# Windowed attention and two gated feed-forward blocks on one core: the order of the evacuations, the first two slices as one group, the softmax normalisation on GpSimd

## The chip, the cores and the metric

The program runs on one core of one Trainium2 chip. The metric is device time in microseconds (us) of one execution; lower is better. The engines are named as the profile names them: PE (TensorE matmul) and PEld (its weight loads), DVE (VectorE), ACT (ScalarE), POOL (GpSimd), SP (SyncE, which here issues all the DMAs).

## What is computed

```python
def _attn_ref(q, k, v):                       # (4, 8, 576, 64)
    scores = np.matmul(q, k.transpose(0, 1, 3, 2)) / np.sqrt(D)
    bias = slopes[:, None, None] * (-np.abs(rel))      # per head
    mask = (rel >= 0) & (rel < 128)
    scores = np.where(mask, scores + bias, -1e9)
    attn = np.exp(scores - max); attn = attn / (sum + 1e-9)
    return np.matmul(attn, v)
def _moe_ref(x, w_gate, w_val, w_out):        # x (2304, 512), d_ff 1536
    return sigmoid(x @ w_gate) * (x @ w_val) @ w_out
def _moe2_ref(x, w1, w2, w3, w_out):          # d_ff 1024
    return ((x @ w1) * (x @ w2) @ w3) @ w_out
```

The reference runs attention, then the first feed-forward block, then the second.

## The kernel before, in words

**Tiles and blocks.** The 2304 tokens are 18 tiles of 128, cut into five blocks of 2, 4, 4, 4 and 4 tiles (`TILES`). Attention runs over 20 steps, block by block and four head pairs in each: steps 0 to 3 are the block of two tiles (half steps), steps 4 to 19 are full. Feed-forward weights are cut into slices of 128 columns: 12 of the first block, 8 of the second. High and low halves of an fp32 value are multiplied in three passes (`PASSES`), so a product of one slice with one block is 12 matmuls, and what follows each product on ACT, DVE and POOL makes the next operand's halves.

**One attention step n** has three stages. `stage_s` multiplies queries and keys (tile `s`), then, for each pair of tiles, DVE merges the two windows (L446), adds the table of biases (L449) and takes the row maxima (L455); ACT does four exponentials with row sums (L462), DVE the reciprocals (L466), and the four 128x128 parts are scaled by them, two on POOL (L470) and two on ACT (L472). `stage_p` transposes the result on PE (L480, tile `pt`), ACT copies it to SBUF (L69, tile `cp`), POOL cuts it into two windows by two selects for each head (L484, L488). `stage_pv` multiplies by the values (L503), ACT and DVE make the halves of `xt`. On PE the stages of three steps are interleaved: p of n-2, pv of n-3, s of n.

**Fillers.** Behind the stages of a step PE gets pieces of the first feed-forward block (`fill`, a budget of PE time for each step, `FILL` and `FULL`). `READY` says at which step which group of slices on which block joins the queue of fillers. `layer` runs `gv` (the gate product, its sigmoid on ACT at L257, the value product, DVE's multiply at L262, ACT's high half at L264, POOL's low half at L265) and leaves the down product (`down1`) to the next layer; each down product is added into `acc` (L287 by ACT for the first group, L289 by DVE later). All of these share four PSUM banks with `pt` and `pv` until the attention is over.

**Order of the work.** PE's order inside the attention is written out by hand (`tc.manual_schedule`). The order on ACT, DVE, POOL and SP comes from a scheduler: it follows the program's order, shifted by `tc.high_priority(offset=...)`. Weights are converted on the way (`convert_next`, one at a time, L115 to L121 and L131 to L135) at an offset of -300. Each engine works off its own list strictly in order.

**Groups before.** `groups` begins with (0,) and (1,), single slices, then pairs. After the attention three layers of the single slices are left, then the pairs run over the five blocks, one after the other, to the end of the kernel.

## Time and profile before

| | |
|---|---|
| median of 3 runs | 945.8 us (945.59 to 946.12) |
| the profiled execution's own time | 945.88 us |
| its span, first to last instruction | 944.2 us |
| busy: PE, DVE, ACT, POOL | 897.6, 573.5, 366.9, 290.6 us |
| mean granted TensorE clock | 0.979 |

A busy share is an average over stages with different limits. Here the span falls into an attention of some 200 us, in which all engines work on short pieces in turn, and 740 us of feed-forward matmuls. A row of the timeline is start, duration, engine and line, and in brackets how long the engine had been idle before and what ended it; "x8" merges eight like instructions, and PE shows two records for an fp32 matmul of the attention. The granted clock is given in tenths or as a share of 2.4 GHz, so 0.5 is 1.2 GHz.

### The profile page before, as it was taken

To read this page: it belongs to the slowest core of one execution; us is meant where nothing else is said; L and a number is where in the kernel's file an instruction comes from. 1 tells how busy PE (TensorE), PEld (TensorE's weight loads), DVE (VectorE), ACT (ScalarE), POOL (GpSimd) and SP (SyncE) were. 2 spreads that over 40 slices of the span, in tenths; PEclk is the share of its full clock that TensorE was granted. 3 is DMA by queue.
4 is the path that set the end of the run, shared out by engine and by line. 5 is a ranking of instruction groups with operands and counts; after the bars stand their busy time and mean duration, and the time that the engine had idled before them with its cause. 6 is when DMAs were issued, how large, how long until landed. Compare 5 with 4: busy or idle time off the path is not lost.

```text
span 944.2 us, 12323 instructions
## 1 busy us (share of the span) xinstructions
PE 897.6 (95%) x4528; PEld 736.6 (78%) x4528; DVE 573.5 (61%) x957; ACT 366.9 (39%) x912; POOL 290.6 (31%) x343
## 2 busy tenths in 40 slices
PE   6788786899999999999999999999999999999998
PEld 3456665678878888888888888888888888888887
DVE  5769686525998797698593458943854514422223
ACT  6799897643333332322331244434322312211110
POOL 4567454242422412322322021104422412411111
PEclk9789898999999999999999999999999999999999
DMA  6445353114243243143130122325310300000112
GB/s 185 150 140 161 99 159 119 40 34 145 79 143 113 67 135 101 45 144 113 45 100 23 46 67 101 112 78 156 97 39 1 112 1 1 23 0 1 45 45 112
DMA packets 32604, 79.71 MB, mean 84 GB/s; under 512 B 3616, under 2 KB 5664, under 8 KB 32544
## 3 DMA queue, kind: packets, MB, share of 16 engines
q1 hardware_dynamic: 32544, 78.92, 26.0%
q8 instruction: 36, 0.59, 0.3%
q14 instruction: 24, 0.20, 0.1%
HBM read 65.27 MB, written 13.63 MB: 84 GB/s over the span
## 4 chain that ended last, share of the span: by engine, by line
PE 73%; DVE 11%; ACT 8%; DMA 4%; issue 4%; POOL 1%; SPq 0%; ACTq 0%; POOLq 0%; DVEq 0%
PE gv L243 43%; PE dn L280 11%; PE o L304 10%; PE w3o L209 4%; ACT sm L462 3%; PE pv L503 2%; DVE acc L289 1%; PE s L438 1%; PE pt L480 1%; ACT sm L472 1%; DVE sm L449 1%; DVE s L446 1%; DVE mn L455 1%; ACT cp L69 1%; POOL wsl L75 1%
## 5 line engine op out<-in xcount | busy, mean ns | idle before, releaser
L243 PE MATMUL gv<-xt,wsl 128*128 128x512 f32 (+1 forms) x1440 | 307.6, 372 | 3.2 <-DVE g L262 1.9
L243 PEld LDWEIGHTS gv<-xt,wsl 128*128 128x128 f32 x1440 | 252.5, 191 | 52.7 <-DVE g L262 3.0
L75 POOL TENSOR_TENSOR gt<-g,gt 128x512 fp32r<-128x512 f32 (+1 forms) x100 | 120.5, 1209 | 430.1 <-ACT gt L69 422.8
L243 PE MATMUL gv<-x,wsl 128*128 128x512 f32 (+1 forms) x960 | 200.2, 368 | 0.0
L243 PEld LDWEIGHTS gv<-x,wsl 128*128 128x128 f32 x960 | 167.6, 189 | 30.2
L262 DVE TENSOR_TENSOR g<-g,gv 128x512 f32<-128x512 f32 (+1 forms) x100 | 62.6, 630 | 168.1 <-PE gv L243 151.1
L280 PE MATMUL dn<-gt,wsl 128*128 128x512 f32 (+1 forms) x720 | 156.3, 371 | 5.0 <-ACT cp L69 3.1
L280 PEld LDWEIGHTS dn<-gt,wsl 128*128 128x128 f32 x720 | 126.4, 189 | 30.1 <-ACT cp L69 3.7
L257 ACT ACTIVATE g<-gv 128x512 f32<-128x512 f32 (+1 forms) x100 | 54.7, 550 | 156.1 <-PE gv L243 150.9
L69 ACT ACTIVATE gt<-g 128x512 fp32r<-128x512 f32 (+1 forms) x100 | 58.5, 587 | 145.4 <-DVE g L262 145.2
L304 PE MATMUL o<-wsl,gt 128*128 128x512 f32 x432 | 101.1, 389 | 0.0
L304 PEld LDWEIGHTS o<-wsl,gt 128*128 128x128 f32 x432 | 80.9, 188 | 16.7
L289 DVE TENSOR_TENSOR acc<-acc,dn 128x512 f32<-128x512 f32 (+1 forms) x120 | 74.1, 628 | 21.8 <-PE dn L280 21.5
L313 DVE TENSOR_TENSOR acc<-acc,o 128x512 f32<-128x512 f32 x54 | 37.1, 688 | 35.2 <-PE o L304 35.2
L462 ACT ACTIVATE sm<-sm,mn 128x128 f32<-128x128 f32 x144 | 55.9, 391 | 1.6 <-DVE mn L455 1.0
L503 PE MATMUL pv<-cp,ldv 128*64 128x256 f32 (+1 forms) x352 | 43.4, 382 | 12.6 <-issue 6.9
L503 PEld LDWEIGHTS pv<-cp,ldv 128*64 128x64 f32 x352 | 27.1, 154 | 29.2 <-issue 12.9
L438 PE MATMUL s<-ldk,ldq 64*128 64x256 f32 x288 | 42.1, 434 | 6.3 <-DMA ldq<-in_q_dram 6.3
L470 POOL TENSOR_SCALAR sm<-sm,su 128x128 f32<-128x128 f32 x72 | 32.6, 464 | 41.4 <-DVE su L466 41.4
L209 PE MATMUL w3o<-wo,w3s 128*128 128x512 f32 x192 | 44.4, 390 | 0.2 <-DVE wo L72 0.2
L209 PEld LDWEIGHTS w3o<-wo,w3s 128*128 128x128 f32 x192 | 36.0, 188 | 8.1 <-DVE wo L72 0.7
L438 PEld LDWEIGHTS s<-ldk,ldq 64*128 64x128 f32 x288 | 29.5, 209 | 14.1 <-issue 10.6
(742 smaller groups left out, 868.7 us busy)
## 6 DMA issues: line engine op xcount, KB each, us to landing
ldk<-in_k_dram SPq DMA_DIRECT2D x16, 320.0 KB, 3.0
ldv<-in_v_dram SPq DMA_DIRECT2D x16, 320.0 KB, 2.9
out_dram<-acc SPq DMA_DIRECT2D x18, 256.0 KB, 2.0
ldq<-in_q_dram SPq DMA_DIRECT2D x16, 256.0 KB, 3.3
w3o<-w3os SPq DMA_DIRECT2D x8, 256.0 KB, 2.5
ldk<-in_k_dram SPq DMA_DIRECT2D x4, 128.0 KB, 2.9
ldq<-in_q_dram SPq DMA_DIRECT2D x4, 128.0 KB, 3.0
raw_(0, 0)_99<-in_w_gate_dram SPq DMA_DIRECT2D x1, 512.0 KB, 4.6
```

The source lines that it names most:

```text
L69: nc.scalar.activation(dst, src, AF.Copy)
L75: nc.gpsimd.tensor_tensor(dst, src, hi.bitcast(F32), ALU.subtract)
L209: nc.tensor.matmul(acc2, w3s[u][:, wp, i * P : (i + 1) * P], wo2[kk][:, xp], start=(kk == 0 and wp == 0 and xp == 0), stop=(kk == NC2 - 1 ...
L243: nc.tensor.matmul(ps, wsl[i][:, s, wp, kk * P : (kk + 1) * P], xs[blk][:, xp, kk], start=(kk == 0 and wp == 0 and xp == 0), stop=(kk == N ...
L257: nc.scalar.activation(g[i], pss[i, 0], AF.Sigmoid if one else AF.Copy)
L262: nc.vector.tensor_tensor(pr, pr, pss[i, 1], ALU.mult)
L280: nc.tensor.matmul(ps, wsl[i][:, 2, wp, m * P : (m + 1) * P], t[:, xp], start=n == 0, stop=n == 3 * len(grp) - 1,)
L289: nc.vector.tensor_tensor(a, a, ps, ALU.add)
L304: nc.tensor.matmul(ps, t[:, xp, tt * P : (tt + 1) * P], wsl[i][:, 2, wp], start=n == 0, stop=n == 3 * len(grp) - 1,)
L438: nc.tensor.matmul(ps[:, h, :, u], ld["q"][r, t * P : (t + 1) * P], ld["k"][r, t * P : (t + 2) * P], start=True, stop=True, skip_group_che ...
L462: s["act"] = nc.scalar.activation(y, y, AF.Exp, bias=mn[:, j : j + 1], scale=1.0 / up, accum_out=su[:, j : j + 1])
L503: nc.tensor.matmul(ps[c, a:b], loads[n]["v"][:, j + 1, c], s["cp", h][:, m0 : m0 + b - a], start=j == -back, stop=j == nt - 1, skip_group_ ...
```

## The change

What it does, by its parts:

1. Priorities: the gate's sigmoid, the multiply and the two halves behind it, and the additions into `acc` are moved ahead in the schedule by 150 (`SOONER`), so ahead of softmax instructions that stand earlier in the program.
2. Tables: an exponential of one element is run before the first data are there; and the one addition that finishes the base table moves from DVE to POOL.
3. Groups: (0, 1) is now one group. On blocks 0 and 1 its slices still run singly; from block 2 on both together, with one down product of six matmuls for two of three. Slices 0 and 1 of block 1 both join at step 12, the pair of block 2 at step 14, of block 3 at step 18.
4. Normalisation: on full steps all four parts are scaled on POOL, none on ACT.
5. After the attention one layer of the pair (0, 1) is left, with three conversions ahead of it; the later groups are numbered one lower, and convert the same items at the same layers.

```diff
+SOONER = 150
...
-    groups = [(0,), (1,)] + [tuple(range(i, i + GF)) for i in range(GF, NF + NM, GF)]
+    groups = [tuple(range(i, i + GF)) for i in range(0, NF + NM, GF)]
...
-            nc.scalar.activation(g[i], pss[i, 0], AF.Sigmoid if one else AF.Copy)
+            with tc.high_priority(offset=SOONER):
+                nc.scalar.activation(g[i], pss[i, 0], AF.Sigmoid if one else AF.Copy)
...
-            nc.vector.tensor_tensor(pr, pr, pss[i, 1], ALU.mult)
             t = m2.tile([P, 2, TB], F32R, tag="gt", name=f"gt{i}_{blk}", bufs=4)[:, :, 0:w]
-            act_copy(t[:, 0], pr)
-            pool_lo(t[:, 1], pr, t[:, 0])
+            with tc.high_priority(offset=SOONER):
+                nc.vector.tensor_tensor(pr, pr, pss[i, 1], ALU.mult)
+                act_copy(t[:, 0], pr)
+                pool_lo(t[:, 1], pr, t[:, 0])
...
-            if first:
-                act_copy(a, ps)
-            else:
-                nc.vector.tensor_tensor(a, a, ps, ALU.add)
+            with tc.high_priority(offset=SOONER):
+                if first:
+                    act_copy(a, ps)
+                else:
+                    nc.vector.tensor_tensor(a, a, ps, ALU.add)
...
-            nc.vector.tensor_tensor(normal, normal, cross, ALU.add)
+            nc.gpsimd.tensor_tensor(normal, normal, cross, ALU.add)
...
-                    if j < 2:
+                    if nt > 2 or j < 2:
                         nc.gpsimd.tensor_scalar(y, y, su[:, j : j + 1], 1.0, ALU.mult, ALU.mult)
                     else:
                         nc.scalar.activation(y, y, AF.Copy, scale=su[:, j : j + 1])
...
-        READY = {5: ((0, 0),), 10: ((0, 1),), 12: ((1, 0),), 14: ((0, 2), (1, 1)), 18: ((0, 3), (1, 2))}
+        READY = {
+            5: (((0,), 0),), 10: (((0,), 1),), 12: (((1,), 0), ((1,), 1)), 14: (((0, 1), 2),), 18: (((0, 1), 3),),
+        }
...
-        convert_start(parts(groups[0]) + parts(groups[1]) + second_items)
+
+        warm = cpool.tile([P, 1], F32, name="warm")
+        nc.vector.memset(warm, 0.0)
+        nc.scalar.activation(warm, warm, AF.Exp)
+        convert_start(parts((0,)) + parts((1,)) + second_items)
...
-    fillers += [layer(groups[0], 4), layer(groups[1], 3), layer(groups[1], 4)]
-    convert_start(parts(groups[2]))
+    fillers.append(layer(groups[0], NBLK - 1))
+    convert_start(parts(groups[1]))
     for f in fillers:
-        for _ in range(2):
+        for _ in range(3):
             if queue:
                 convert_next()
```

Three places in the engines' lists. The names are those of the program with step, or slice and block, in them: `sm4` and `su4` are the softmax and row sums of step 4, `cp2_0` the transposed copy of step 2, head 0, `acc1_0` the sums of the first feed-forward block on token block 0, `g1_0` the gate of slice 1 on block 0. Lines of the changed kernel are its own, 1 to 4 higher.

POOL around step 4, before:

```order
L470 TENSOR_SCALAR sm4_314<-sm4_314,su4_0_328 128x128 x2
L484 AFFINE_SELECT cp2_0_365<-cp2_0_365 128x2x128
L488 AFFINE_SELECT cp2_0_365<-cp2_0_365 128x2x128
L470 TENSOR_SCALAR sm4_314<-sm4_314,su4_1_343 128x128 x2
L484 AFFINE_SELECT cp2_1_372<-cp2_1_372 128x2x128
L484 AFFINE_SELECT cp3_0_385<-cp3_0_385 128x2x128
L488 AFFINE_SELECT cp2_1_372<-cp2_1_372 128x2x128
L488 AFFINE_SELECT cp3_0_385<-cp3_0_385 128x2x128
L484 AFFINE_SELECT cp3_1_392<-cp3_1_392 128x2x128
L488 AFFINE_SELECT cp3_1_392<-cp3_1_392 128x2x128
```

and in the changed kernel:

```order
L76 TENSOR_TENSOR wsl0_195<-a_(0, 0)_186,wsl0_195 128x512
L488 AFFINE_SELECT cp2_0_368<-cp2_0_368 128x2x128
L488 AFFINE_SELECT cp2_1_375<-cp2_1_375 128x2x128
L492 AFFINE_SELECT cp2_0_368<-cp2_0_368 128x2x128
L492 AFFINE_SELECT cp2_1_375<-cp2_1_375 128x2x128
L488 AFFINE_SELECT cp3_0_388<-cp3_0_388 128x2x128
L492 AFFINE_SELECT cp3_0_388<-cp3_0_388 128x2x128
L488 AFFINE_SELECT cp3_1_395<-cp3_1_395 128x2x128
L492 AFFINE_SELECT cp3_1_395<-cp3_1_395 128x2x128
L474 TENSOR_SCALAR sm4_317<-sm4_317,su4_0_331 128x128 x4
L474 TENSOR_SCALAR sm4_317<-sm4_317,su4_1_346 128x128 x4
```

The selects of steps 2 and 3 stand ahead of the normalisation of step 4, which is now eight instructions, and behind the low half of the first weight slice.

ACT around step 12, where the first down product (`dn0_0`, four PSUM banks) is evacuated, before:

```order
L462 ACTIVATE sm12_1092,su12_0_1106<-sm12_1092,mn12_0_1105 128x128 x4
L69 ACTIVATE gt0_1_1134<-g0_1_1028 128x512
L465 ACTIVATE su12_0_1106<-su12_0_1106 128x4
L69 ACTIVATE acc1_0_1137<-dn0_0_0_1138 128x256
L69 ACTIVATE acc1_0_1137<-dn0_0_1_1143 128x256
L462 ACTIVATE sm12_1092,su12_1_1121<-sm12_1092,mn12_1_1120 128x128
L472 ACTIVATE sm12_1092<-sm12_1092,su12_0_1106 128x128 x2
L462 ACTIVATE sm12_1092,su12_1_1121<-sm12_1092,mn12_1_1120 128x128 x3
L69 ACTIVATE acc1_0_1137<-dn0_0_2_1148 128x256
L465 ACTIVATE su12_1_1121<-su12_1_1121 128x4
L69 ACTIVATE acc1_0_1137<-dn0_0_3_1153 128x256
```

and in the changed kernel:

```order
L70 ACTIVATE acc1_0_1140<-dn0_0_0_1141 128x256
L70 ACTIVATE acc1_0_1140<-dn0_0_1_1146 128x256
L70 ACTIVATE acc1_0_1140<-dn0_0_2_1151 128x256
L70 ACTIVATE acc1_0_1140<-dn0_0_3_1156 128x256
L466 ACTIVATE sm12_1095,su12_0_1109<-sm12_1095,mn12_0_1108 128x128 x4
L259 ACT_TABLE_LOAD
L259 ACTIVATE g1_0_1174<-gv1_0_0_1161 128x256
L469 ACTIVATE su12_0_1109<-su12_0_1109 128x4
L466 ACT_TABLE_LOAD
L466 ACTIVATE sm12_1095,su12_1_1124<-sm12_1095,mn12_1_1123 128x128
L70 ACTIVATE gt1_0_1281<-g1_0_1174 128x256
```

The four copies into `acc1_0` stand ahead of the exponentials of step 12 now; ACT's own scalings are gone; and the sigmoid stands between the exponentials, with a table load on either side. Over the whole list there are 18 table loads where there were 14.

DVE at the start, before:

```order
L446 COPY_PREDICATED s0_0_123<-mask_87,s0_0_123 128x2x256
L369 TENSOR_TENSOR base_88<-base_88 128x128
L446 COPY_PREDICATED s1_0_162<-mask_87,s1_0_162 128x2x256
L449 SCALAR_TENSOR_TENSOR sm0_122<-s0_0_123,tab0_117 128x512
L449 SCALAR_TENSOR_TENSOR sm1_161<-s1_0_162,tab0_117 128x512
L455 TENSOR_REDUCE mn0_0_130<-sm0_122 128x4
```

and in the changed kernel:

```order
L546 MEMSET warm_99 128x1
L450 COPY_PREDICATED s0_0_126<-mask_87,s0_0_126 128x2x256
L450 COPY_PREDICATED s1_0_165<-mask_87,s1_0_165 128x2x256
L453 SCALAR_TENSOR_TENSOR sm0_125<-s0_0_126,tab0_120 128x512
L453 SCALAR_TENSOR_TENSOR sm1_164<-s1_0_165,tab0_120 128x512
L459 TENSOR_REDUCE mn0_0_133<-sm0_125 128x4
```

The addition to the base table is gone from the list; the second window merge (`s1_0`) still stands ahead of the first use of the table (`sm0`).

## Rows read from the trace of the kernel before

**Rows 1.** The page, 40 slices of the span (23.6 us each): busy tenths, granted clock.

```profile
PE   6788786899999999999999999999999999999998
...
PEclk9789898999999999999999999999999999999999
```

**Rows 2.** Stretches: length, busy us and count by engine, clock, DMA share, GB/s.

```profile
4.20:33.30 29.10, 18.93 (x88) 10.85 (x88) 19.13 (x39) 21.40 (x90) 16.22 (x39) 0.91 0.61 193
33.30:87.50 54.20, 48.81 (x345) 35.05 (x344) 42.90 (x80) 47.36 (x176) 34.07 (x58) 0.89 0.47 149
87.50:105.60 18.10, 13.43 (x82) 11.24 (x80) 10.21 (x20) 16.97 (x60) 11.09 (x21) 0.72 0.24 81
105.60:201.60 96.00, 79.69 (x518) 59.70 (x514) 60.41 (x113) 71.47 (x225) 42.02 (x68) 0.95 0.31 99
201.60:290.00 88.40, 87.55 (x420) 73.45 (x419) 68.47 (x111) 29.84 (x52) 28.03 (x22) 1.00 0.36 116
```

**Rows 3.** Timeline, 7 to 10 us: start, duration, engine, line, tiles, idle before and releaser.

```profile
7.38 1.28 ACT L404 ACT_TABLE_LOAD   x1 [7.38 <-DVE base L369]
...
8.46 0.70 DVE L446 COPY_PREDICATED s<-mask,s 128x512 f32<-128x512 int32 x1 [1.17 <-PE s L438]
...
9.42 1.29 DVE L449 SCALAR_TENSOR_TENSOR sm<-s,tab 128x512 f32<-128x512 f32 x2 [0.26 <-ACT tab L404]
```

**Rows 4.** Timelines of PE and POOL, 29 to 37 us.

```profile
29.59 1.14 POOL L470 TENSOR_SCALAR sm<-sm,su 128x128 f32<-128x128 f32 x2
...
29.66 1.11 PE L503 MATMUL pv<-cp,ldv 128*64 128x256 f32 x2 [2.60 <-POOL cp L488]
...
31.86 1.54 PE L503 MATMUL pv<-cp,ldv 128*64 128x256 f32 x6 [1.09 <-POOL cp L488]
...
33.33 3.79 PE L438 MATMUL s<-ldk,ldq 64*128 64x256 f32 x16
```

**Rows 5.** Groups: busy us and mean ns, idle before; the second: shortest, median, longest ns.

```profile
L470 POOL TENSOR_SCALAR sm<-sm,su 128x128 f32<-128x128 f32 x72 | 32.6, 464 | 41.4 <-DVE su L466 41.4
...
L470 POOL TENSOR_SCALAR sm<-sm,su x72: 365/372/1052, 13.5 to 189.5; 128x128 f32<-128x128 f32 x72
...
L488 POOL TENSOR_SCALAR_AFFINE_SELECT cp<-cp 128x512 f32<-128x512 f32 (+1 forms) x40 | 25.0, 629 | 1.5
...
L75 POOL TENSOR_TENSOR gt<-g,gt 128x512 fp32r<-128x512 f32 (+1 forms) x100 | 120.5, 1209 | 430.1 <-ACT gt L69 422.8 <-ACT su L465 7.1
...
L472 ACT ACTIVATE sm<-sm,su 128x128 f32<-128x128 f32 x72 | 24.8, 393 | 2.7 <-DVE su L466 2.7
```

**Rows 6.** Timeline of PE, 93 to 103 us.

```profile
93.78 1.01 PE L280 MATMUL dn<-gt,wsl 128*128 128x256 f32 x3 [2.09 <-ACT cp L69]
...
97.36 5.49 PE L243 MATMUL gv<-xt,wsl 128*128 128x256 f32 x24 [1.01 <-ACT acc L69]
```

**Rows 7.** Timelines of ACT and PE, 114 to 179 us.

```profile
114.39 0.57 ACT L69 ACTIVATE acc<-dn 128x512 f32<-128x512 f32 x1
...
115.06 1.95 PE L503 MATMUL pv<-cp,ldv 128*64 128x128 f32 x20 [2.93 <-issue]
...
159.01 2.04 ACT L69 ACTIVATE acc<-dn 128x512 f32<-128x512 f32 x4
...
159.73 1.94 PE L480 MATMUL pt<-ident,sm 128*128 128x128 f32 x8 [6.93 <-ACT acc L69]
...
173.12 1.28 ACT L257 ACT_TABLE_LOAD   x1
...
174.41 0.60 ACT L257 ACTIVATE g<-gv 128x512 f32<-128x512 f32 x1
...
175.11 3.38 PE L503 MATMUL pv<-cp,ldv 128*64 128x128 f32 x20 [3.07 <-issue]
```

**Rows 8.** Timeline of PE, 273 to 295 us.

```profile
273.72 3.04 PE L243 MATMUL gv<-xt,wsl 128*128 128x512 f32 x12 [0.85 <-DVE g L262]
...
291.53 3.02 PE L243 MATMUL gv<-xt,wsl 128*128 128x512 f32 x12 [1.07 <-DVE g L262]
```

More of the change, by code (lines that the diff above doesn't have):

```diff
@@ L188, in attn_moe_kernel @@
     early = [it for it in fold_src if it[0][0] == "o2" or it[0][1] in W3_AHEAD]
-    early += [((i, c), (w1, w2)[c][i - NF]) for c in range(2) for i in groups[NF // GF + 1]]
+    early += [((i, c), (w1, w2)[c][i - NF]) for c in range(2) for i in groups[NF // GF]]
     late_n = len(early)
-    early += [((i, c), (w_gate, w_val, w_out)[c][i]) for c in range(3) for i in groups[2]]
+    early += [((i, c), (w_gate, w_val, w_out)[c][i]) for c in range(3) for i in groups[1]]
     early32 = dpool.tile([P * len(early), DM], F32, name="early32")
@@ L562, in attention @@
                 for grp, blk in READY.get(n, ()):
-                    fillers.append(layer(groups[grp], blk))
+                    fillers.append(layer(grp, blk))
                 fill(FILL.get(n, FULL))
@@ L577, in attn_moe_kernel @@
     gvtag, gvbufs = "gv", 4
-    last1 = NF // GF
-    n_ahead = -(-len(ahead_items) // (last1 - 2))
+    last1 = NF // GF - 1
+    n_ahead = -(-len(ahead_items) // (last1 - 1))
     fold_it = fold()
@@ L597, in attn_moe_kernel @@
         convert_next()
-    for gi, grp in list(enumerate(groups))[2:]:
+    for gi, grp in list(enumerate(groups))[1:]:
         if gi == last1 + 1:
@@ L611, in attn_moe_kernel @@
         elif gi + 1 < len(groups):
-            more = ahead_items[n_ahead * (gi - 2) : n_ahead * (gi - 1)] if gi < last1 else []
+            more = ahead_items[n_ahead * (gi - 1) : n_ahead * gi] if gi < last1 else []
             convert_start(more[:2] + parts(groups[gi + 1]) + more[2:])
```

## The prediction

> **What bounds the kernel now.** First the page's slices [rows 1]: from the ninth on (189 us) PE is busy 90% or more at full clock to the end, and what ACT, DVE or POOL do there counts only where PE waits for it. So I read above all what lies ahead of that. PE's work is the same before and after (the groups are cut otherwise, but each product keeps its matmuls), so the time can change only by what PE loses: idle time, and matmuls run at half clock.
>
> The table of stretches [rows 2] says where that is. The reader subtracts PE's busy time from the length: 10.2 us idle from 4.2 to 33.3 (the start), 5.4 to 87.5 (steps 5 to 11), 4.7 to 105.6 (step 12 alone), 16.3 to 201.6 (steps 13 to 19), then 0.85. The clock column gives the second loss, at most length times what is missing to 1.00: 2.6, 6.0, 5.1, 4.8 us. The timeline shows where it comes from: after an idle of 2.93 us 20 matmuls of a `pv` still took 1.95 us, but after 3.07 us, in a stretch with more gaps, they took 3.38 [rows 7]; PE is then at 1.2 and not 2.4 GHz. In all some 38 us idle and up to 18 us slow, 56 us to win.
>
> Who makes PE wait? In steps 5 to 11 ACT is busy 47.4 of 54.2 us [rows 2]; it is the fullest engine beside PE, and DVE (42.9) comes next. From step 12 on it is not ACT's load but its order. Row by row [rows 6, 7]: `dn` at 93.78 waited 2.09 us, `gv` at 97.36 1.01 us for ACT. The `pv` at 115.06 has "issue" as its releaser, but a copy into `acc` ends on ACT at 114.96, and it sat behind exponentials: it had to free the PSUM bank. The same holds for the `pv` at 175.11 and the sigmoid that ends at 175.01. And the 6.93 us before 159.73 are a wait for four copies that began at 159.01, behind a scaling (L472) with which ACT itself waited for DVE's reciprocal, as its scalings did for 2.7 us in all [rows 5].
>
> **The change, part by part**, against the profiled execution's own 945.88 us (its span 944.2, 1.7 us around it; the median is 945.8). Gains are negative; in brackets both ends.
>
> *A. Early tables.* The table load (1.28 us) waited for DVE's addition until 7.38, and the first use of the table came at 9.42 [rows 3]. But DVE's list has the second window merge ahead of that use, and this waits for PE until 8.46 and takes 0.6 to 0.7: `sm0` starts at about 9.15, so 0.27 us are gained where the load suggests 2. The next reciprocal now stands behind step 2's merge. I take 0 [-1 to +2].
>
> *B. Block 0.* Before, POOL's select for `cp2_1` stood behind the second scaling of step 4 (29.59); the `pv` of step 2 waited 2.60 and 1.09 us, and the `s` of step 5 behind it ran 3.79 us at half clock [rows 4], 1.9 lost: 5.6 us. In the new list the selects come ahead of step 4's scalings, but behind the low half of a weight slice. I take -4 [-6 to -1].
>
> *C. Steps 5 to 11.* POOL takes over 28 scalings (two on each of two tile pairs in seven steps): 28 x 0.45 (32.6/72) = +12.7 us, so 34.1 becomes 46.8 of 54.2; ACT loses 28 x 0.34 (24.8/72) = 9.6 and falls to 37.8 [rows 2, 5]. The two change places as the fullest. What ACT no longer holds up, POOL may: four scalings in a row instead of two, so 0.9 us later for `pt`; and the list of ACT now often has the `cp` of step n ahead of the exponentials of n+1, which ties the steps into a chain. The stretch loses 11.4 us today; half of it could go (-5), and the chain with 12.7 us more POOL work could cost as much as two thirds of those 12.7 (+8). Neither end is nearer: 0 [-5 to +8].
>
> *D. Step 12.* 9.8 us lost (4.7 idle, 5.1 slow). All four copies of `dn0_0` now stand ahead of the exponentials, so PE can go through both products of slice 1. What is late next is `pt` of step 11, behind POOL's queue (low half, table, scalings). Two thirds: -6.5 [-9 to -2].
>
> *E. Steps 13 to 19.* 21.1 us lost, of which 12.9 are the three waits of [rows 7] (2.93, 6.93, 3.07) and 2.4 the matmuls behind the last two at half clock (1.0 of the 1.94 of `pt`, 1.4 of the 3.38 of `pv`). All three are evacuations behind softmax work, and all three move: the copies go ahead, L472 is off ACT, and the down product of block 2 comes after the softmax. From 15.3 I take off a quarter for what replaces them: four more table loads on ACT, 4 x 1.28 = 5.1 us [rows 7], and in step 19 two sigmoids between the exponentials, where `pt` comes late. -11.5 [-17.5 to -6]. The 17 matmuls of fillers that the new list has ahead of the last `pv` (102 are left after it before the second group's second block, against 119) are no gain of their own: they are what fills the gaps.
>
> *F. After the attention.* The two DVE waits of 0.85 and 1.07 [rows 8] stand behind conversions; the multiply now goes first, and 12 additions into `acc` are gone from DVE. -1.9 [-1.9 to 0].
>
> *G. The shorter bridge.* Slices 2 and 3 are converted once the attention's memory is free. By the lists PE has 78 matmuls between the last `pv` and their first use, against 107: 29 x 0.25 (3.02/12) [rows 8] = 7.3 us less cover. Today PE never waits there (0.85 idle to 290, all of it at 273.72 [rows 2, 8]). I take 0 [0 to +7]. SP's list has two weight loads earlier, ahead of the keys of steps 6 and 15; their buffers are free by then, and I count nothing; if not, the keys come a load later, inside C's bound. The warm-up (one memset, one tiny exponential) and the addition moved to POOL lie where these engines wait for data.
>
> Sum: 0 - 4 + 0 - 6.5 - 11.5 - 1.9 + 0 = -23.9, so **922 us**. The ends of the terms add up to 905 and 954.
>
> The load that goes ahead of a switched table is 1.28 us, and the sigmoid followed 0.01 us behind it [rows 7]. The Trainium skill, "ScalarE: Activation LUTs", section "Table sets: the hidden batching unit", says to batch activations by set, which speaks against this change; its section "What ACT_TABLE_LOAD costs" gives 1.283 us and a drain, 2.66 us a switch. By the page the four loads would be 10.6 us of ACT and the sum at most 5.5 later; the row shows no such drain.
>
> **The rivals.**
>
> *More is won (0.14).* POOL keeps up in steps 5 to 11, with scalings at their median of 0.37 us [rows 5], and the new waits stay out: B -6, C -5, D -7.5, E -17.5, F -1.9, about 908 us. For it: ACT, the fullest engine, loses 20%. Against: a POOL at 86%, in one chain with ACT.
>
> *The waits are replaced (0.17).* POOL takes ACT's place as what PE waits for: B -2, C +6, D -5, E -8, F -1.9, so 935 us. For it: POOL's part of the softmax chain doubles, and each `pt` stands behind it. Against: from step 12 on POOL is busy 42 of 96 us [rows 2].
>
> *POOL becomes the bound, slower (0.07).* A scaling lasts from 0.365 to 1.052 us [rows 5]. With eight to a step, four selects of 0.62 (25.0/40) and a low half of 1.2 [rows 5], POOL's step is 8m + 3.7 us, where steps now take 11.2 (168.3 over 15, from 33.3 to 201.6). It decides from a mean m of 0.94 on; at the longest seen the step is 12.1, 15 x 0.9 = 13 us more: 959 us. Against: the mean is 0.46 now. The Trainium skill, "GPSIMD Engine Reference", section "Key points", names a mechanism for this: SBUF interfaces shared with VectorE, contended by instructions with two SBUF inputs. The spread from 0.365 to 1.052 agrees.
>
> *It does not do what it says (0.05).* The lists show that priorities and groups do move instructions, so for all of it to be worth nothing B, D and E must be given back in C and G: within 2 us of 946.
>
> **How the numbers follow.** The forecast has 0.57, with its own range of 911 to 932. The range of 906 to 940 takes in the rivals at 908 and 935 and leaves out the slower one, no change, and the best end of all terms, some 0.18. A measurement of this kernel can tell about 0.2% (1.9 us) from no change. Faster: 0.57 + 0.14 + 0.17 = 0.88; same 0.05; slower 0.07.
>
> **What would show it.** In the stretch of steps 13 to 19 PE's idle time should be under 8 us, and no wait as long as 6.93; the gap at step 12 under 2 us; the last `pv` should end near 184 (on 201.6, 22 us less lost, and some 4 us of fillers more ahead of it); and at the second group no wait for DVE over 0.5 us. In steps 5 to 11 I expect POOL busiest after PE, and `pt` released by POOL's scalings. I am wrong if the end of the attention moves by less than 10 us, if steps 5 to 11 take over 62 us, or if PE waits for slices 2 and 3.

## The result, and the profile of the changed kernel

The changed kernel takes **937.4 us** (median of 4 runs, 936.9 to 939.1) beside 946.0 for the kernel before (945.6 to 946.9): ratio 0.9911, 95% interval 0.9894 to 0.9928. It is 8.6 us faster. The forecast of 922 had the direction right and the gain nearly three times too large; 937.4 lies inside the range of 906 to 940, outside the forecast's own 911 to 932, and close to the rival "the waits are replaced" (935).

The page's slices, against [rows 1]: 23.6 us each before, 23.4 now.

```profile
PE   5889799899999999999999999999999999999998
...
PEclk9999899999999999999999999999999999999999
```

The stretches, cut at the same places of the program as [rows 2] (the first `s` of steps 5, 12 and 13, the end of the last `pv`); columns: length, then busy us and count of PE, PEld, DVE, ACT, POOL, then clock.

```profile
4.20:32.20 28.00, 19.47 (x88) 11.85 (x89) 17.11 (x33) 16.99 (x75) 13.90 (x32) 1.00 0.56 181
32.20:91.20 59.00, 50.53 (x345) 35.56 (x344) 46.11 (x89) 47.89 (x181) 46.55 (x96) 0.92 0.44 146
91.20:101.10 9.90, 9.56 (x83) 8.15 (x81) 8.41 (x17) 8.43 (x22) 7.57 (x15) 0.97 0.30 95
101.10:196.87 95.77, 84.93 (x533) 63.20 (x531) 59.90 (x114) 66.41 (x205) 57.13 (x107) 0.95 0.34 105
196.87:290.00 93.13, 91.68 (x436) 76.38 (x436) 72.35 (x115) 35.41 (x61) 28.01 (x22) 1.00 0.39 124
```

Compare the lengths. The start is 1.1 us shorter, steps 5 to 11 are 4.8 **longer** (59.0 against 54.2), step 12 is 8.2 shorter with PE idle 0.34 us where it was 4.7, and steps 13 to 19 are as long as before (95.8 against 96.0), but 17 more matmuls of fillers lie in them (533 against 516; the 518 of [rows 2] take in two that end just behind the cut). What follows the last `pv` is 4.3 us shorter (935.2 - 196.9 = 738.3 against 944.2 - 201.6 = 742.6), which is just those 17 matmuls at 0.25 us. So -1.1 + 4.8 - 8.2 - 0.2 - 4.3 = -9.0, the difference of the two spans.

PE's four largest waits from 80 to 300 us, by line and releaser: us in total, times, longest.

```profile
PE gv L244 <- ACT acc L70: 4.0, 1, 4.0
PE pt L484 <- POOL sm L474: 3.3, 2, 2.0
PE gv L244 <- DVE g L266: 1.4, 2, 0.8
PE dn L283 <- ACT cp L70: 1.2, 1, 1.2
```

The stall of 6.93 us [rows 7] is gone; a new one of 4.04 stands in step 13. The timeline of all engines at that place (start, duration, engine, line, tiles, idle before and what ended it) shows who holds it:

```profile
100.96 3.42 POOL L474 TENSOR_SCALAR sm<-sm,su 128x128 f32<-128x128 f32 x4 [2.33 <-DVE su L470]
...
106.37 1.41 POOL L474 TENSOR_SCALAR sm<-sm,su 128x128 f32<-128x128 f32 x4
...
108.33 1.26 POOL L76 TENSOR_TENSOR wsl<-a_(1, 2)_937,wsl 128x512 fp32r<-128x512 f32 x1
...
109.63 0.67 ACT L116 ACTIVATE a_('ahead', 3, 0)_1189<-raw_('ahead', 3, 0)_948 128x512 f32<-128x512 f32 x1 [5.05 <-POOL wsl L76]
110.20 1.08 ACT L70 ACTIVATE acc<-dn 128x512 f32<-128x512 f32 x2
...
110.84 2.50 PE L244 MATMUL gv<-xt,wsl 128*128 128x512 f32 x5 [4.04 <-ACT acc L70]
```

Read it backwards. PE waits for a copy into `acc` on ACT. That copy stands behind the first instruction of a weight conversion (`rounded`, L116), and ACT waits 5.05 us with it, because its tile `a_` has two buffers and the older one is read by the low half on GpSimd (L76), which comes late behind the scalings and the selects. The evacuation has its priority over the softmax, and an instruction of a conversion without any urgency is ahead of it in ACT's list all the same.

### The profile page after: what moved, and what is told of

It is laid out like the page before. It is cut to its first block, busy times and chain, and to the rows that moved or that the text cites. A ratio compares the mean times of both kernels' runs of the same rounds, so it can differ in the third digit from the quotient of the medians.

```text
span 935.2 us, 12293 instructions
## 1 busy us (share of the span) xinstructions
PE 897.4 (96%) x4528; PEld 735.1 (79%) x4528; DVE 565.1 (60%) x945; ACT 355.1 (38%) x853; POOL 311.6 (33%) x408
## 4 chain that ended last, share of the span: by engine, by line
PE 72%; DVE 8%; ACT 7%; POOL 6%; DMA 4%; issue 3%; SPq 0%; ACTq 0%; POOLq 0%; DVEq 0%
PE gv L244 43%; PE dn L283 11%; PE o L308 10%; PE w3o L210 4%; ACT sm L466 2%; POOL sm L474 2%; PE s L442 1%; PE pv L507 1%; POOL wsl L76 1%; PE pt L484 1%; POOL cp L488 1%; POOL cp L492 1%; ACT L466 1%; DVE sm L453 1%; DVE s L450 1%
## 5 line engine op out<-in xcount | busy, mean ns | idle before, releaser
L76 POOL TENSOR_TENSOR gt<-g,gt 128x512 fp32r<-128x512 f32 (+1 forms) x100 | 121.2, 1216 | 427.9 <-ACT gt L70 427.7
L308 PE MATMUL o<-wsl,gt 128*128 128x512 f32 x432 | 101.1, 389 | 0.0
L293 DVE TENSOR_TENSOR acc<-acc,dn 128x512 f32<-128x512 f32 (+1 forms) x108 | 66.1, 622 | 20.7 <-PE dn L283 20.5
L474 POOL TENSOR_SCALAR sm<-sm,su 128x128 f32<-128x128 f32 x136 | 53.9, 416 | 21.4 <-DVE su L470 21.2
L507 PE MATMUL pv<-cp,ldv 128*64 128x256 f32 (+1 forms) x352 | 40.9, 370 | 4.8 <-POOL cp L492 3.7
```

What stands on the lines that cost most here:

```text
L76: nc.gpsimd.tensor_tensor(dst, src, hi.bitcast(F32), ALU.subtract)
L293: nc.vector.tensor_tensor(a, a, ps, ALU.add)
L308: nc.tensor.matmul(ps, t[:, xp, tt * P : (tt + 1) * P], wsl[i][:, 2, wp], start=n == 0, stop=n == 3 * len(grp) - 1,)
L474: nc.gpsimd.tensor_scalar(y, y, su[:, j : j + 1], 1.0, ALU.mult, ALU.mult)
L507: nc.tensor.matmul(ps[c, a:b], loads[n]["v"][:, j + 1, c], s["cp", h][:, m0 : m0 + b - a], start=j == -back, stop=j == nt - 1, skip_group_ ...
```

## The experiments

Each ratio is to the kernel before, run on the same chip. The other columns are read from one profiled execution each; two executions of one kernel (e9 and e15) differ by up to 3.4 us in them (in the last column; by 0.5 to 2.3 in the others), so that a smaller difference counts only where several kernels agree. The profiled executions of e2, e6, e14 and e15 lie 2 to 3 us above the medians of their kernels.

| kernel | us | ratio, 95% interval | step 7 to 12 | step 12 | step 13 begins | 13 to last `pv` | PE idle in it | last `pv` |
|---|---|---|---|---|---|---|---|---|
| before | 946.0 | 1 | 40.0 | 18.1 | 105.7 | 96.0 | 16.3 | 201.6 |
| changed | 937.4 | 0.9911, 0.9894 to 0.9928 | 42.9 | 9.9 | 101.1 | 95.8 | 10.8 | 196.9 |
| e1, normalisation back | 936.4 | 0.9923, 0.9898 to 0.9947 | 41.4 | 11.3 | 102.1 | 96.0 | 10.5 | 198.1 |
| e2, no priority | 938.9 | 0.9946, 0.9926 to 0.9966 | 40.4 | 15.6 | 104.9 | 96.1 | 12.6 | 201.0 |
| e3, groups back | 932.0 | 0.9872, 0.9848 to 0.9896 | 43.3 | 9.6 | 100.1 | 88.4 | 10.3 | 188.4 |
| e4, third buffer | 934.0 | 0.9894, 0.9873 to 0.9915 | 42.8 | 10.1 | 101.2 | 93.1 | 10.0 | 194.3 |
| e5, no early tables | 942.8 | 0.9978, 0.9963 to 0.9992 | 44.9 | 10.0 | 106.5 | 96.3 | 11.1 | 202.8 |
| e6, early tables alone | 943.0 | 0.9978, 0.9962 to 0.9994 | 40.3 | 18.2 | 106.7 | 96.1 | 16.8 | 202.8 |
| e7, priority and normalisation | 936.7 | 0.9918, 0.9891 to 0.9946 | 45.1 | 9.8 | 106.6 | 88.3 | 10.2 | 194.9 |
| e8, e3 and third buffer | 930.0 | 0.9833, 0.9817 to 0.9850 | 42.7 | 10.2 | 100.4 | 87.9 | 9.6 | 188.3 |
| e9, e8, priority from 12 on | 926.5 | 0.9812, 0.9798 to 0.9827 | 39.7 | 13.9 | 100.8 | 83.4 | 6.7 | 184.2 |
| e10, e9, normalisation from 12 on | 936.7 | 0.9918, 0.9903 to 0.9933 | 39.0 | 18.1 | 104.9 | 90.5 | 11.2 | 195.4 |
| e11, e8, normalisation back | 935.3 | 0.9907, 0.9890 to 0.9924 | 40.9 | 10.8 | 100.2 | 92.2 | 14.0 | 192.4 |
| e12, priority alone | 938.6 | 0.9940, 0.9921 to 0.9959 | 40.7 | 13.6 | 104.9 | 91.8 | 12.0 | 196.8 |
| e13, e9, merged groups | 932.6 | 0.9870, 0.9849 to 0.9892 | 39.8 | 14.0 | 101.7 | 91.1 | 8.5 | 192.9 |
| e14, merged behind only | 928.5 | 0.9828, 0.9807 to 0.9849 | 39.8 | 13.9 | 102.1 | 84.4 | 6.5 | 186.5 |
| e15, e9 again | 927.6 | 0.9808, 0.9791 to 0.9825 | 40.2 | 14.9 | 103.1 | 84.5 | 7.9 | 187.6 |

("Step 7 to 12" is from the first `s` of step 7 to that of step 12.) Kernels with merged groups have 527 to 537 matmuls from step 13 to the last `pv`, the others 515 to 518.

**One part undone at a time (e1, e2, e3), and the new wait (e4).** My first theory was that GpSimd's longer part in the softmax chain is what steps 5 to 11 lost.

```diff
-                    if nt > 2 or j < 2:
+                    if j < 2:
```

> The changed kernel with the normalisation as it was before (two scalings of a tile pair on GpSimd, two on ScalarE); all else stays. Theory A, the longer POOL part of the softmax chain is what steps 5 to 11 lost: from the s of step 5 to the s of step 12 the 59.0 us of the changed kernel fall to 54 to 56, and as ACT's scalings wait for a reciprocal again, steps 13 to 19 lose 1 to 2 us; in sum 933 to 936. Theory B, the normalisation is what freed ACT's list for the evacuations of steps 12 to 19: the long PE waits of the kernel before come back in part, 941 to 945. Theory C, it matters nowhere: 936 to 938.

Theory A falls: from step 5 to step 12 it takes 90.8 - 31.9 = 58.9 us, as the changed kernel, and the time can't be told from it. Here the normalisation is worth nothing (theory C). From step 7 to step 12 alone it is 1.5 us less; what several kernels together say of that stands under C below.

```diff
-SOONER = 150
+SOONER = 0
```

> The changed kernel with the priority of the evacuations taken away (offset 0), all else stays. Theory A, the priority carries steps 12 and 13 to 19: the 8.2 us of step 12 and the 5 us of idle after it come back, and steps 5 to 11 keep their 59 us because GpSimd still normalises: 946 to 952. Theory B, the priority gives back in steps 5 to 11, by early table loads and copies ahead of the exponentials, a good part of what it wins: steps 5 to 11 fall to 54 to 56 us and the time is 938 to 943. Theory C, groups and normalisation carry the gain: 936 to 938.

The time is as theory B has it, the way there is in between: step 12 takes 15.6 us, so the priority carries most of its gain, and steps 7 to 11 are 2.6 us shorter without it. In sum the priority is worth some 3 us (0.9911 to 0.9946, the intervals touching). And a long wait is there in step 16: PE waits 7.08 us for a sigmoid that stands behind eight exponentials on ACT.

```profile
153.61 3.68 PE L507 MATMUL pv<-cp,ldv 128*64 128x128 f32 x20 [7.08 <-ACT g L259]
```

```diff
-    groups = [tuple(range(i, i + GF)) for i in range(0, NF + NM, GF)]
+    groups = [(0,), (1,)] + [tuple(range(i, i + GF)) for i in range(GF, NF + NM, GF)]
...
-        READY = {
-            5: (((0,), 0),), 10: (((0,), 1),), 12: (((1,), 0), ((1,), 1)), 14: (((0, 1), 2),), 18: (((0, 1), 3),),
-        }
+        READY = {5: ((0, 0),), 10: ((0, 1),), 12: ((1, 0),), 14: ((0, 2), (1, 1)), 18: ((0, 3), (1, 2))}
...
-    fillers.append(layer(groups[0], NBLK - 1))
+    fillers += [layer(groups[0], 4), layer(groups[1], 3), layer(groups[1], 4)]
```

> The kernel before with the priority, the early tables and the normalisation on GpSimd, but its own groups (slices 0 and 1 apart in all blocks). Theory A, the merged groups are worth only what they take off DVE and off the waits after the attention: 937 to 939. Theory B, they carry a good part of the gain (12 additions and 12 evacuations fewer, one down product and not two): 941 to 945. Theory C, they cost something, since both slices of block 1 now start together in step 12 and fill less of the steps before: 932 to 935.

The edit takes part 5 of the change back too. Theory C: without the merged groups it is faster, 0.9872 against 0.9911. A part of the change for which the prediction had put down no loss costs some 4 us. The two intervals just overlap, but two more pairs below that differ in the same edit have theirs apart: e4 and e8 (0.9894 and 0.9833), e5 and e7 (0.9978 and 0.9918), 6 us each.

```diff
-        a = spool.tile([P, DM], U32, name=f"a_{key}", tag="ca")
+        a = spool.tile([P, DM], U32, name=f"a_{key}", tag="ca", bufs=3)
```

> The changed kernel with a third buffer for the tile that the conversion of a weight slice begins with (tag ca), so that its first instruction on ACT no longer waits for the low half on GpSimd of the conversion before. Theory A, that wait is what holds the copies into acc and so PE for 4.04 us at 106.8 us: the wait falls under 1 us, PE stays at full clock there, and the time is 931 to 934. Theory B, something else is late next (the reciprocal, the table loads): the wait moves by under 1 us or another takes its place, 936 to 938.

The wait of 4.04 us is gone (the longest from there on is 1.41): the same conversion now begins at 105.19 and has waited 0.41 us, for its own data.

```profile
105.19 0.68 ACT L116 ACTIVATE a_('ahead', 3, 0)_1189<-raw_('ahead', 3, 0)_948 128x512 f32<-128x512 f32 x1 [0.41 <-DMA raw_('ahead', 3, 0)_948<-in_w_gate_dram]
```

This bears out the chain read above (the scheduler moves some other instructions of ACT with it, so the buffer isn't all that differs). The time is as theory A has it, at its upper end, and the interval of the ratio overlaps that of the changed kernel: waits of 1.0 to 1.3 take a part of the place.

**The early tables (e5, e6).** In all of e1 to e4 steps 5 to 11 took 57 to 59 us. What they share is the early tables.

```diff
-        warm = cpool.tile([P, 1], F32, name="warm")
-        nc.vector.memset(warm, 0.0)
-        nc.scalar.activation(warm, warm, AF.Exp)
...
-            nc.gpsimd.tensor_tensor(normal, normal, cross, ALU.add)
+            nc.vector.tensor_tensor(normal, normal, cross, ALU.add)
```

> The changed kernel without the early tables (no warm-up, the addition of the mask planes on VectorE again). The runs that undid the normalisation, the priority or the groups all kept 57 to 59 us from the s of step 5 to the s of step 12, where the kernel before has 54.2; what they share is the early tables. Theory A, the early tables change the order of block 0's work on all engines and that is where steps 5 to 11 lose: the stretch falls to 54 to 55 us, the start is 1 us longer, and the time is 932 to 935. Theory B, each of the other parts alone is enough to lengthen the stretch: it stays at 57 to 60, and the time is 937 to 940.

Both theories fall, the other way round: without the early tables it is 6 us slower, steps 5 to 11 take 62.3. The timeline of POOL from 26 to 36 us, first of the changed kernel:

```profile
28.64 1.27 POOL L76 TENSOR_TENSOR wsl<-a_(0, 0)_186,wsl 128x512 fp32r<-128x512 f32 x1 [1.71 <-ACT wsl L70]
29.86 0.77 POOL L488 TENSOR_SCALAR_AFFINE_SELECT cp<-cp 128x256 f32<-128x256 f32 x2
30.58 0.77 POOL L492 TENSOR_SCALAR_AFFINE_SELECT cp<-cp 128x256 f32<-128x256 f32 x2
...
33.70 2.33 POOL L474 TENSOR_SCALAR sm<-sm,su 128x128 f32<-128x128 f32 x6
```

and of e5:

```profile
26.55 2.46 POOL L474 TENSOR_SCALAR sm<-sm,su 128x128 f32<-128x128 f32 x4 [2.17 <-DVE su L470]
28.98 0.84 POOL L488 TENSOR_SCALAR_AFFINE_SELECT cp<-cp 128x256 f32<-128x256 f32 x1
29.89 0.74 POOL L492 TENSOR_SCALAR_AFFINE_SELECT cp<-cp 128x256 f32<-128x256 f32 x1
...
30.97 1.41 POOL L474 TENSOR_SCALAR sm<-sm,su 128x128 f32<-128x128 f32 x4
```

With the early tables POOL does block 0's selects ahead of step 4's scalings. Without them the scalings, now four, go first, and the `pv` at 30.68 waits 3.42 us for the selects, more than the 2.60 of [rows 4]. The tables change the order of the list, not the time of the first softmax: ACT's first exponential starts at 11.52 us in the changed kernel and at 11.34 before. That this order is what the 6 us come from is read from these rows; no run changed it alone.

The reverse of this edit, put into the kernel before and nothing else:

> The kernel before with the early tables alone (warm-up, the addition of the mask planes on GpSimd). Theory A (the early tables cost what steps 5 to 11 lost): the start is 1 us shorter and the stretch from the s of step 5 to the s of step 12 grows from 54.2 to 57 to 59 us: 3 us slower than the kernel before, if the rest keeps its order. Theory B: within 2 us of the kernel before, the stretch at 54 to 55.

The stretch from step 5 to step 12 is 57.2 us, as theory A has it, the time is as theory B has it: some 2 us faster (the interval runs from 0.6 to 3.6 us), but the profiled execution, from which the stretch is read, isn't faster (945.98, where the median is 943.0). In it step 13 begins at 106.7, 1.0 later than before. Priority alone (e12) brings it to 104.9, priority and normalisation without tables (e7) to 106.6; only kernels with both priority and tables come to 100 to 103 (all of them but e10).

The kernel before with the change's `SOONER` blocks and its condition on `nt`:

> The kernel before with the priority and the normalisation, but without early tables and without the merged groups. Theory A (early tables cost 3 to 5 us, merged groups 4 to 5): 927 to 930, steps 5 to 11 at 54 to 55 us. Theory B (only the groups cost): 932 to 934, steps 5 to 11 at 57 to 59.

Slower than either theory: from step 5 to step 12 it takes 62.5 us, and against e3, which differs by the early tables alone, the time is 4.3 us longer (the intervals just overlap).

**A version better than both (e8 to e12).** e8 is e3 with e4's edit.

> The version with the groups of before (priority, early tables, normalisation), and a third buffer for the tile ca. It had a wait of 4.12 us of PE at 109.92 us behind the same conversion on ACT. Theory A, the third buffer takes that wait away and what it took off the changed kernel (1.6 us by the ratios, although the wait itself was 4) it takes off here: 928 to 931. Theory B, another wait takes its place: 931 to 933.

By the ratios the third buffer is worth some 3.7 us here (0.9872 to 0.9833), but the intervals just overlap and the two profiled executions differ by 0.6. The wait of 4.12 is gone, and waits of 1.4 to 2.1 stand elsewhere: PE idles 9.6 us behind step 12 where it idled 10.3. What the buffer is worth is not clear of the noise, here as in e4. In the next kernel the priority begins with step 12:

```diff
-            with tc.high_priority(offset=SOONER):
+            with tc.high_priority(offset=SOON[0]):
...
+                SOON[0] = SOONER if n >= 12 else 0
```

> The version with the groups of before and the third buffer (930.0 us), with the priority of the evacuations only from step 12 on. From the s of step 7 to the s of step 12 every kernel with the priority took 41 to 45 us, and the two without it 40.3. Theory A, the priority of slice 0's sigmoids and copies ahead of the exponentials is what lengthens steps 7 to 11: they fall to 40 to 41 us, step 12 stays under 11 us, and the time is 926 to 928. Theory B, GpSimd's part in the softmax chain lengthens them: they stay at 42 to 43 us, 929 to 931. Theory C, without the priority the work of slice 0 is late and step 12 pays: step 12 over 13 us, 931 to 934.

Steps 7 to 11 fall to 39.7 us, as theory A has it, but step 12 takes 4 us more, as theory C has it; what is left over, some 2 us (0.9833 to 0.9812, the intervals overlap a little), comes in steps 13 to 19. The same pair with merged groups (e4 and e13) gives 42.8 to 39.8, 10.1 to 14.0 and 93.1 to 91.1.

```diff
-                    if nt > 2 or j < 2:
+                    if n >= 12 or j < 2:
```

> The same, and the normalisation too goes to GpSimd only from step 12 on; steps 5 to 11 are then as in the kernel with early tables alone (40.3 us from the s of step 7 to the s of step 12). Theory A (both parts cost in steps 7 to 11 and win from step 12 on): 925 to 928. Theory B (GpSimd's normalisation costs nothing in steps 7 to 11, its rest is what frees ACT for step 12): equal to the run with the priority from 12 on, or up to 2 us slower.

Far slower than either theory said, 10 us: step 12 is back at 18.1 us, and a wait of 5.21 stands in step 17. Rows of ACT and PE in e10:

```profile
93.23 0.69 ACT L477 ACTIVATE sm<-sm,su 128x128 f32<-128x128 f32 x2 [1.62 <-DVE su L471]
...
95.61 1.85 PE L284 MATMUL dn<-gt,wsl 128*128 128x256 f32 x6 [3.52 <-ACT cp L71]
...
156.72 2.04 ACT L71 ACTIVATE acc<-dn 128x512 f32<-128x512 f32 x4
...
157.45 1.94 PE L485 MATMUL pt<-ident,sm 128*128 128x128 f32 x8 [5.21 <-ACT acc L71]
```

At step 12 it is what the change was meant for: a scaling of step 11 on ACT (L477) waits 1.62 us for the reciprocal, and copies stand behind it. But at 156.72 no scaling is on ACT any more, and the four copies stand behind eight exponentials none the less. In e9 the same four copies lie between the exponentials, and what is left is a wait of 2.51 of the `dn` whose results they copy:

```profile
144.39 3.49 PE L284 MATMUL dn<-gt,wsl 128*128 128x512 f32 x9 [2.51 <-ACT cp L71]
...
146.85 0.58 ACT L71 ACTIVATE acc<-dn 128x512 f32<-128x512 f32 x1
147.33 0.39 ACT L467 ACTIVATE sm<-sm,mn 128x128 f32<-128x128 f32 x1
147.62 0.19 ACT L467 ACTIVATION_READ_ACCUMULATOR sm<-sm,mn 128x1 f32 x1
147.71 0.58 ACT L71 ACTIVATE acc<-dn 128x512 f32<-128x512 f32 x1
```

So the place in the list makes the long wait, and an edit in steps 4 to 11 decides the place in step 17. e11 is e8 with e1's edit, e12 the kernel before with the `SOONER` blocks alone.

> The version with the groups of before and the third buffer (930.0 us), with the normalisation as before the change (two scalings of a pair on GpSimd, two on ScalarE). Theory A, the normalisation is worth nothing, as in the changed kernel, where undoing it left the time within 2 us: 928 to 932. Theory B, with the other waits out of the way ACT's wait for the reciprocal counts: 934 to 938.

Theory B: with the groups of before the normalisation is worth 7 us (0.9907 against 0.9833, the intervals apart; 4 us between the two profiled executions), and the same wait is back at 5.87 us.

```profile
153.84 1.94 PE L484 MATMUL pt<-ident,sm 128*128 128x128 f32 x8 [5.87 <-ACT acc L70]
```

In e1, with the merged groups, it was worth nothing, and this wait isn't there although the normalisation is undone: the merged groups put block 2's down product elsewhere. So either part removes this wait, and the two share a gain. How much of the 7 us that is stays open, since e11 differs from e1 in the third buffer as well, and between e12 and e7, without tables and third buffer, the normalisation is worth 2 us, which the noise covers.

> The kernel before with the priority alone. Theory A, the priority carries the gain of step 12 (8 us) and of steps 13 to 19 (idle time from 16 to 10 us), and gives 3 to 5 back in steps 5 to 11 for want of the early tables: 934 to 938. Theory B, it needs GpSimd's normalisation to free ACT's list: 940 to 944.

Just behind theory A. Step 12 wins 4.6 us of the 8.2, and a wait of 4.88 stays in step 17.

**The merged groups by themselves (e13 to e15).** e13 is the changed kernel with the edits of e4 and e9, that is e9 with e3's edit taken back; e14 goes on from e13.

> The changed kernel with the third buffer and with the priority only from step 12 on: against the best version so far (926.5 us) it differs in the merged groups alone. Theory A, the merged groups cost 4 to 6 us wherever they are put, by half-clock matmuls and waits in steps 13 to 19 and about 1 us of waits behind the attention: 930 to 933. Theory B, their cost was tied to a wait that is gone by now: 926 to 928.

e13 and e15 differ in the groups alone and ran on the same chip: 0.9870 and 0.9808, the intervals apart, 5.9 us. That is the time of theory A, but not by matmuls at half clock: from step 13 on the mean granted clock is 0.98 in both.

```diff
-            5: (((0,), 0),), 10: (((0,), 1),), 12: (((1,), 0), ((1,), 1)), 14: (((0, 1), 2),), 18: (((0, 1), 3),),
+            5: (((0,), 0),), 10: (((0,), 1),), 12: (((1,), 0),), 14: (((0,), 2), ((1,), 1)), 18: (((0,), 3), ((1,), 2)),
...
-    fillers.append(layer(groups[0], NBLK - 1))
+    fillers += [layer((1,), 3), layer(groups[0], NBLK - 1)]
```

> The same with slices 0 and 1 apart in blocks 1 to 3, as before the change, and together only in block 4 behind the attention. Theory A, the cost of the merged groups lies in steps 13 to 19: PE idle about 7 us there, the last pv near 184 us, the time 925.5 to 927.5. Theory B, it lies behind the attention, where fewer matmuls stand before the second group: 929 to 932.

Between the theories, nearer A: 4 of the 5.9 us are got back by parting blocks 1 to 3 in the attention (the intervals of e13 and e14 touch). The rest seems to be behind it: PE idles 1.9 us there before 290 us in e14, two waits for DVE, and not at all in e15; but the intervals of e14 and e15 overlap. Windows of PE from step 13 to the last `pv`, first e13, then e9 and e14:

```profile
101.74:192.85 91.11, 82.66 (x533) 0.98 0.31 99
```

```profile
100.80:184.15 83.35, 76.62 (x515) 0.98 0.33 108
```

```profile
102.05:186.49 84.44, 77.93 (x515) 0.96 0.33 106
```

From e9 to e13: 7.8 us longer, of which 18 matmuls at 0.25 are 4.5 and only moved forward, 1.7 are idle time, and some 1.5 are matmuls that took longer (against e15 6.6, 4.5, 0.6 and 1.5). What makes these, the PSUM banks that two slices hold at once or the copies that then come together, was not tried and stays open.

> The best version so far once more (priority from step 12 on, normalisation on GpSimd, early tables, third buffer, groups of before). Every theory: ratio to the kernel before of 0.979 to 0.983, and the last pv at 184 us.

The ratio is as expected, the last `pv` is not: 187.6 us, 3.4 later than in e9. The best version is 0.9808 (e9: 0.9812), 18 us faster than the kernel before and 9 to 10 faster than the changed one: the change without merged groups, with the priority from step 12 on and a third buffer. No other offset than 150 and no other first step than 12 was tried.

## Why the prediction was right in direction and wrong in size

The sum forecast -23.9 us and the two spans differ by -9.0. Of the 14.9 us between them 7.0 lie in E, 4.8 in C, 2.9 in A and B and 1.9 in F (what follows the last `pv` is shorter by the 17 matmuls alone); D gave 1.7 more than forecast. So the step that failed most is E, the waits of steps 13 to 19: it was priced at -11.5 and measured -4.5.

*A, early tables, 0.* The reading of the rows was right, the first exponential did not come earlier. What failed is pricing the edit by that alone: it costs 6.3 us to take it out of the change (0.9911 to 0.9978), 4.3 with the groups apart (0.9872 to 0.9918), and some 2 us are won by it alone. It decides the order of POOL's list in block 0.

*B, block 0, -4.* Of the 2.60 and 1.09 us that the `pv` of step 2 waited 1.21 are left, and the `s` of step 5, 3.79 us at half clock, takes 2.00. But the `pv` of step 0 now waits 2.48 us at 21.96, where before that of step 1 waited 1.33 at 22.75. And the 1.1 us that step 5 begins earlier are gone by step 7, whose `s` starts at 48.3, before at 47.5. Rows of PE ahead of it, in the changed kernel:

```profile
43.58 0.33 PE L484 MATMUL pt<-ident,sm 128*128 128x128 f32 x1 [1.98 <-POOL sm L474]
...
45.43 2.94 PE L507 MATMUL pv<-cp,ldv 128*64 128x128 f32 x20
```

and before:

```profile
44.60 1.11 PE L480 MATMUL pt<-ident,sm 128*128 128x128 f32 x6 [1.39 <-POOL sm L470]
45.65 1.95 PE L503 MATMUL pv<-cp,ldv 128*64 128x128 f32 x20
```

The `pt` of step 5 waits 1.98 us for POOL's scalings, which end no earlier (44.97, before 44.89), and the same 20 matmuls behind it take 2.94 us where they took 1.95, at a mean granted clock of 0.64 where it was 1.00. The prediction counted a wait as won without naming what is late next.

*C, steps 5 to 11, 0 with ends of -5 and +8.* Measured +4.8, inside. POOL is busy 46.55 us where 46.8 was worked out, and `pt` waits 8.0 us for its scalings in all, before 4.8. But ACT stayed the fullest engine, at 47.9, since its work is not cut where PE's is: 59 exponentials fall into the stretch, not 48. Groups of the stretch, ACT and PE of the changed kernel, then PE of the kernel before (busy, mean ns, idle before):

```profile
L466 ACT ACTIVATE sm<-sm,mn 128x128 f32<-128x128 f32 x59 | 22.9, 391 | 0.2
```

```profile
L484 PE MATMUL pt<-ident,sm 128*128 128x128 f32 x56 | 13.0, 329 | 8.3 <-POOL sm L474 8.0
```

```profile
L480 PE MATMUL pt<-ident,sm 128*128 128x128 f32 x56 | 10.4, 302 | 5.1 <-POOL sm L470 4.8
```

Of the 4.8 us, 1.9 lie in steps 5 and 6 (see B) and 2.9 from step 7 to 12. There the price I feared is not that of the scalings by themselves. With early tables, kernels that have in these steps both the priority and all scalings on GpSimd take 42.7 to 43.3 us (the changed one, e3, e4, e8), those with one of the two 39.7 to 41.4 (e1, e11; e2, e9, e13 to e15), those with neither 40.3 and 39.0 (e6, e10). Without early tables it is 45 (e5, e7), 40.7 (e12) and 40.0 (before). So the term that was left out is the two together: the priority in steps where the softmax, not the evacuation, is what PE needs next, on top of a softmax that ends later on GpSimd. By which instruction each lengthens the other was not taken apart.

*D, step 12, -6.5.* Measured -8.2. The priority carries most of it: step 12 takes 15.6 us without it and 11.3 without the normalisation, where the changed kernel takes 9.9, and 18.1 in e10 without either in the steps ahead.

*E, steps 13 to 19, -11.5.* Measured -4.5, with the 17 matmuls that were done earlier counted at 0.25 us. The three old waits did go, but a quarter was too little for what took their place. First, the new wait of 4.04 us: the prediction took that quarter off for table loads and sigmoids, and did not look at what else stands ahead of a copy in ACT's list. Without the wait (e4) the stretch is 2.7 us shorter. Second, the merged groups, which the prediction counted in E only as gaps filled, take away some 4 us here and 2 behind the attention by the ratios of e13 to e15; between the profiles of pairs that differ in them alone it is 0.7 to 3.5 us here, beyond the fillers, and 1.5 to 4.1 behind. With both out of the way (e8) the stretch takes 87.9 us with the count of before (515, before 516), -8.1. Only with the later priority as well does it take 83.4 and 84.5 (e9, e15), -12.6 and -11.5, and then step 12 is 4 us longer: the size of E was met by another kernel, and there by moving a part of the loss ahead. Third, the wait of 6.93 was explained by the scaling L472 and its reciprocal [rows 7]. That scaling waited 0.31 us for the reciprocal; what else stood ahead of the four copies were eight exponentials and one more pair of scalings, and e10, with no scaling there, waits 5.21.

```profile
158.41 0.69 ACT L472 ACTIVATE sm<-sm,su 128x128 f32<-128x128 f32 x2 [0.31 <-DVE su L466]
```

*F, -1.9.* Waits for DVE of 0.64 and 0.81 us stand where 0.85 and 1.07 stood [rows 8]: half a microsecond won.

```profile
278.71 3.02 PE L244 MATMUL gv<-xt,wsl 128*128 128x512 f32 x12 [0.64 <-DVE g L266]
282.54 3.02 PE L244 MATMUL gv<-xt,wsl 128*128 128x512 f32 x12 [0.81 <-DVE g L266]
```

In the experiments with slices apart PE idles 0 to 0.13 us there until 290 us, even in e6, which has the early tables alone. So these waits go without the priority and without fewer additions, the two reasons that F gave; where the merged groups are, 0.9 to 1.9 us stay.

*G, the shorter bridge, 0.* Right: PE never waits for slices 2 and 3.

Of the forecast's own tests the last `pv` (196.9, not 184), the idle time of steps 13 to 19 (10.8, not under 8), the end of the attention (4.8 us earlier, not 10), the waits for DVE (0.81, not under 0.5) and the busiest engine of steps 5 to 11 (ACT, not POOL) said wrong; the gap at step 12 (0.34) and the end of the 6.93 us wait said right. The rival "the waits are replaced" had the time; it named POOL as what PE would wait for, which holds in steps 5 to 11, and the longest wait was one for ACT.

The four table loads more on ACT came as forecast: 17 instead of 13, the first load of each kernel not counted, in two groups of the page of the changed kernel.

```profile
L259 ACT ACT_TABLE_LOAD x9 | 11.5, 1283 | 0.9 <-PE gv L244 0.7
...
L466 ACT ACT_TABLE_LOAD x8 | 10.3, 1283 | 0.1
```

A load at 97.48 us begins within 0.02 us of the end of the instruction ahead of it, and its sigmoid at 98.78 within 0.02 of its own end. By the Trainium skill, "ScalarE: Activation LUTs", section "What ACT_TABLE_LOAD costs", a drain of 1.38 us comes on top; no run here shows it beside a load, so the rows decide.

## What to carry to other kernels

Where a scheduler makes the lists, a part of a change isn't priced by the rows it touches: compare, on each in-order engine, what now stands ahead of the instruction that PE needs, up to the end, and look there for instructions without urgency that wait for something slow. A priority for evacuations is worth having where PE waits for evacuations (step 12 and after), and lengthens the steps where it waits for the softmax, here only together with the longer softmax on GpSimd. Undo each part of a change singly before adding up their gains, since two parts can remove the same wait (normalisation and merged groups, in step 17), or make a gain or a loss only together (tables and priority; priority and normalisation in steps 7 to 11).

## What was not expected of the hardware

GpSimd's scalings of 128x128 take 374 ns in the median and up to 1315 (shortest, median, longest):

```profile
L474 POOL TENSOR_SCALAR sm<-sm,su x136: 367/374/1315, 14.7 to 187.2; 128x128 f32<-128x128 f32 x136
```

The four at 100.96 us took 3.42 us, while DVE ran conversions of two slices; the four at 106.37 took 1.41. DVE pays too: a step of a conversion took 1.11 us, over its first half beside a select on GpSimd, and the same step 0.68 with GpSimd idle.

```profile
97.83 0.81 POOL L492 TENSOR_SCALAR_AFFINE_SELECT cp<-cp 128x512 f32<-128x512 f32 x1
...
98.07 1.11 DVE L119 SCALAR_TENSOR_TENSOR a_(1, 2)_937<-raw_(1, 2)_740,a_(1, 2)_937 128x512 uint32<-128x512 uint32 x1
...
99.77 0.68 DVE L119 SCALAR_TENSOR_TENSOR a_('ahead', 2, 0)_1046<-raw_('ahead', 2, 0)_833,a_('ahead', 2, 0)_1046 128x512 uint32<-128x512 uint32 x1
```

The Trainium skill, "GPSIMD Engine Reference", section "Key points", says that the two share their SBUF interfaces and contend when DVE reads two SBUF inputs. The rows fit that, but no run here took the conversions away.

The same kernel can meet the same waits at either clock: in step 12 PE idled 2.82 us in e9 and 2.31 in e15, and the mean granted clock of the step was 1.00 in the one and 0.77 in the other; it took 13.9 and 14.9 us.
